# Attention output and half of the normalised input transposed by DMA in place of TensorE, with query blocks of 112

## The chip, the cores and the metric

The kernel runs on one core of one Trainium2 chip. The metric is device time in microseconds (us); lower is better. The kernel before took a median of 177.43 us over three runs (176.70 to 177.52).

## What is computed

One layer over 2048 tokens of width 448, all in bf16. The input is normalised, and two branches read the normalised rows `xn`: a sliding, dilated attention with 16 heads of 28, and a dense layer of width 1792 with gelu. The second gates the first.

```python
xn = (x - mean(x)) / sqrt(var(x) + 1e-5)
q, k, v = split_heads(xn @ wqkv)                      # 16 heads of 28
# query s sees the keys s, s-2, s-4, ..., s-14 that are not negative
s = (softmax(q . k[idx] / sqrt(28)) @ v[idx]).merge_heads() @ wo
h = gelu(xn @ w1 + b1) @ w2 + b2                      # 448 -> 1792 -> 448
out = x + s * silu(h)
```

## The kernel before, in words

Since the window steps by two, even and odd tokens never meet in the attention. The kernel lays the tokens out as two halves, first the 1024 even ones and then the 1024 odd ones (`tok`, `rows`), so that a query sees 8 neighbouring positions. All work is done in this order of tokens: 16 tiles of 128 tokens, grouped into four chunks of 512.

**The work of a tile or chunk.** A tile is loaded, its statistics are taken (`stats`, `rstds`), and VectorE writes the normalised rows into an `xn` buffer (`norm`, L359). The matmuls need the width on the partitions, so TensorE transposes each tile with four matmuls against an identity (L366), and VectorE or ScalarE copies the result from PSUM into `xnT`. From `xnT` come, chunk by chunk, q and k (`qk`, L415 and L418), and the hidden layer `h` (`ff1`, L457 and L460, gelu by ScalarE at L464). `vproj` (L435, L438) makes v for the 128 keys of one attention block. The width 448 is three times 128 and a rest of 64, and the second line number of each pair is the matmul for that rest.

**An attention block** (`attn`) holds 120 queries, the first one 128, against 128 keys; there are 17. TensorE makes the scores of 16 heads in 16 small matmuls (L526) into four PSUM banks, ScalarE takes exp (L532), VectorE multiplies by a mask (L540), and TensorE multiplies with v (L547, 16 matmuls in four groups of four), where a column of ones gives the sum. VectorE takes the reciprocal `rd` (L554) and writes the scaled output `os` (L559). Then TensorE transposes `os` with four matmuls of 112 columns (L568), and VectorE or ScalarE copies the result into `oT` (through the helper `copy`, L258 and L260). One block holds the border between the halves and has a mask of its own (`m_sp`).

**The end of a tile.** `ff2` multiplies `h` with `w2` (L483, 14 matmuls in two groups of seven), VectorE and ScalarE form the gate `g`, and `final` multiplies `oT` with `wo` (L584, four matmuls), scales and adds (L589, L594) and stores the tile through SyncE's queue (L598).

**What sets the order.** The kernel writes no order by hand. `_Plan` collects every step with its engine, an assumed cost, what it depends on, a priority and the buffers it takes; `run` then simulates these costs, and `emit` issues the steps in the order of that simulated time. Each engine, and the queue of DMAs that SyncE issues, runs its steps strictly in this order. Where a step may run on two engines (the copies), the plan also chooses the engine. The stages are added as: chunk 0's gelu layer (F), attention of chunks 0 and 1 (A), F of 1, A of 2, F of 2, A of 3, F of 3. Steps of `ff2`, `qk`, `vproj` and `final` fill the gaps between. Warm-up matmuls (L273) keep TensorE busy until the first weights are there. The bias `b1` comes in as 14 rows, `b1r`, is turned by one matmul (L625) and copied (L629); its load stands behind the hold `t_hold` in SyncE's queue, after the loads of `w1`.

Of the kernel before, what the change touches and what calls it, by code (L numbers as in the profile page):

```python
# [143 lines left out]
def kernel(  # L144
# [26 lines left out]
    GW = 4 * DH  # L171
# [3 lines left out]
    BLK = [(0, 128, 0)] + [(128 + 120 * i, 120, 120 + 120 * i) for i in range(16)]  # L175
    SPLIT = next(i for i, (q0, n, _) in enumerate(BLK) if q0 <= HALF < q0 + n)

# [16 lines left out]

    x_sb = sb("x_sb", [P, NT, D])
# [7 lines left out]
    wo = sb("wo", [P, G, D])  # L203
# [6 lines left out]
    oT = sb("oT", [P, G, S])  # L210
    ident = sb("ident", [P, P])
    eps_t = sb("eps_t", [P, 1], F32)
    m_gen = sb("m_gen", [P, 4, 120])
    m_b0 = sb("m_b0", [P, 4, 128])
    m_sp = sb("m_sp", [P, 4, 120])
    m1 = [sb(f"m1_{i}", [P, 128]) for i in range(3)]
# [7 lines left out]
    p_xn = ring("xn", 3, [P, 512])  # L224
# [3 lines left out]
    p_os = ring("os", 2, [P, D])  # L228
# [19 lines left out]
    def act(n):  # L248
        return 0.19 + n / 1200.0
# [37 lines left out]
    t_E = [plan.add("DVE", 0.08, memset("vector", e[:, :, 120:], 0.0), [t_on], prio=95) for e in p_E.bufs]  # L287

    def dma(eng, dst, src, kb, prio, deps=()):
        def fn(_):  # L290
            (nc.sync if eng == "SP" else nc.scalar).dma_start(dst, src)  # L291
# [63 lines left out]
    def norm(t, prio):  # L355
        def f1(k):
            xn = buf(p_xn, k)
            for o, i in ((xn[:, :D], x_sb[:, t, :]), (xn[:, D:], x_sb[:, t, KF:])):
                nc.vector.tensor_scalar(o, i, mv[:, t, 0:1], rstd[:, t:t + 1], op0=ALU.subtract, op1=ALU.mult)  # L359

        a = plan.add("DVE", 0.45, f1, [t_rs[t]], prio, take=(p_xn,))

        def f2(k):
            xn, tp = buf(p_xn, a), half_bank(buf(p_b, k))
            for kt in range(KT):
                nc.tensor.transpose(tp[:, kt, :], xn[:, kt * P:(kt + 1) * P], ident[:])  # L366
# [149 lines left out]
    def attn(b, prio, gate, early):  # L516
        q0, nq, k0 = BLK[b]
        m = m_b0 if b == 0 else m_sp if b == SPLIT else m_gen
# [39 lines left out]
        def f6(k):  # L558
            nc.vector.tensor_tensor(  # L559
                out=buf(p_os, k)[:nq, :].rearrange("p (h c) -> p h c", h=H),  # L560
                in0=buf(p_b, po)[:nq, :].rearrange("p (h c) -> p h c", h=H)[:, :, :DH],
                in1=buf(p_rd, r)[:nq, :].unsqueeze(2).to_broadcast((nq, H, DH)), op=ALU.mult)
        o = plan.add("DVE", dve(D), f6, [r], prio + 4, take=(p_os,), give=((p_b, po, 0), (p_rd, r, 0)))

        def f7(k):
            tp, os_ = half_bank(buf(p_b, k)), buf(p_os, o)
            for g in range(G):
                nc.tensor.transpose(tp[:GW, g, :nq], os_[:nq, GW * g:GW * (g + 1)], ident[:nq, :nq])  # L568
        tr = plan.add("PE", 0.21, f7, [o], prio + 4, take=(p_b,), give=((p_os, o, 0),), tail=0.15)

        def f8(k):
            copy(k.on, oT[:GW, :, q0:q0 + nq], half_bank(buf(p_b, tr))[:GW, :, :nq])
        t_oT[b] = plan.add(("DVE", "ACT"), (dve(4 * nq, 2), act(4 * nq)), f8, [tr], prio + 4,
                           give=((p_b, tr, 0),))
# [3 lines left out]
    def final(t, prio):  # L578
        deps = [t_oT[b] for b, (q0, nq, _) in enumerate(BLK) if q0 < (t + 1) * P and q0 + nq > t * P]

        def f1(k):
            ps = buf(p_b, k)
            for g in range(G):
                nc.tensor.matmul(ps[:, :D], oT[:GW, g, t * P:(t + 1) * P], wo[:GW, g, :],  # L584
                                 start=(g == 0), stop=(g == G - 1))
        a = plan.add("PE", pe(D, G), f1, deps + t_wo + [t_f2[min(t + 1, NT - 1)]], prio, take=(p_b,), tail=0.15)
# [26 lines left out]
    t_b1r = dma("SP", b1r[:], B_b1.rearrange("(m f) -> m f", f=P), 4, 87, [t_hold])  # L613
# [4 lines left out]
    t_wo = [dma("SP", wo[:GW, :, :], A_wo.rearrange("(g p) c -> p g c", p=GW), 392, 80, [t_hold])]  # L618
# [7 lines left out]
    a = plan.add("PE", 0.3, f1, [t_b1r, t_ident], 97, take=(p_b,), tail=0.15)  # L626
# [38 lines left out]
    project(0)  # L665
    project(1)
# [57 lines left out]
```

## Time and profile before

| | |
|---|---|
| median of three runs | 177.43 us |
| the profiled execution's own time | 178.15 us |
| its span, first to last instruction | 176.4 us |
| TensorE (PE) busy | 168.8 us, 96% |
| ScalarE (ACT) busy | 113.2 us, 64% |
| VectorE (DVE) busy | 112.4 us, 64% |
| mean granted TensorE clock | 0.993 |
| DMA | 9.12 MB, mean 52 GB/s |

The profile is of one execution, taken by the hardware profiler. The span is 1.75 us shorter than the execution's own time. PE is the matmul row, PEld the weight loads that overlap it, SPq is the queue of instructions on SyncE that issue DMAs. A line such as L366 is a line of the kernel. "Idle before" is how long the engine sat idle just before an instruction, and the arrow names what ended that. The chain of waits is followed back from the last instruction, at each step to what released it or to the instruction before it on its engine.

### The profile page before, as it was taken

To read this page: it belongs to the slowest core of one execution; us is meant where nothing else is said; L and a number is where in the kernel's file an instruction comes from. 1 tells how busy PE (TensorE), PEld (TensorE's weight loads), DVE (VectorE), ACT (ScalarE), POOL (GpSimd) and SP (SyncE) were. 2 spreads that over 40 slices of the span, in tenths; PEclk is the share of its full clock that TensorE was granted. 3 is DMA by queue.
4 is the path that set the end of the run, shared out by engine and by line. 5 is a ranking of instruction groups with operands and counts; after the bars stand their busy time and mean duration, and the time that the engine had idled before them with its cause. 6 is when DMAs were issued, how large, how long until landed. Compare 5 with 4: busy or idle time off the path is not lost.

```text
span 176.4 us, 3588 instructions
## 1 busy us (share of the span) xinstructions
PE 168.8 (96%) x1442; PEld 84.6 (48%) x1442; DVE 112.4 (64%) x305; ACT 113.2 (64%) x202; POOL 3.1 (2%) x16
## 2 busy tenths in 40 slices
PE   7998899999999999999999999999999999999990
PEld 2465335444555455434465544344565543455540
DVE  5699771877699779710699964002799892055663
ACT  2356679798847779779954289696965948811120
POOL 7000000000000000000000000000000000000000
PEclk9999999999999999999999999999999999999997
DMA  5999960000000000000101000000000010001001
GB/s 141 323 351 222 373 192 4 4 0 2 4 0 0 4 0 4 26 0 0 32 8 37 13 24 0 6 0 0 26 4 26 4 52 0 0 30 50 30 26 52
DMA packets 8604, 9.12 MB, mean 52 GB/s; under 512 B 588, under 2 KB 8076, under 8 KB 8588
## 3 DMA queue, kind: packets, MB, share of 16 engines
q1 hardware_dynamic: 7740, 8.21, 15.1%
q10 hardware_dynamic: 848, 0.69, 1.4%
q8 instruction: 11, 0.18, 0.5%
q14 instruction: 5, 0.04, 0.1%
HBM read 7.06 MB, written 1.84 MB: 50 GB/s over the span
## 4 chain that ended last, share of the span: by engine, by line
PE 86%; DMA 9%; DVE 2%; SPq 1%; issue 1%; DVEq 0%
PE bank L483 24%; PE bank L457 21%; PE bank L415 9%; PE bank L584 7%; PE bank L435 6%; DMA b1r<-in_B_b_dram 5%; PE bank L547 4%; PE bank L460 4%; DMA wraw<-in_A_wqkv_dram 3%; PE bank L526 3%; PE bank L568 3%; PE bank L418 2%; PE bank L366 1%; PE bank L438 1%; SPq L291 1%; DVE sg L589 1%
## 5 line engine op out<-in xcount | busy, mean ns | idle before, releaser
L483 PE MATMUL bank<-w,h 128*128 128x448 bf16 x224 | 46.8, 352 | 0.0
L464 ACT ACTIVATE h<-bank,b 128x512 bf16<-128x512 f32 x56 | 34.7, 688 | 8.7 <-PE bank L460 8.5
L457 PE MATMUL bank<-xnT,w 128*128 128x512 bf16 x168 | 39.1, 380 | 0.0
L532 ACT ACTIVATE E<-bank 128x480 bf16<-128x480 f32 (+1 forms) x68 | 33.3, 582 | 8.1 <-PE bank L526 8.1
L483 PEld LDWEIGHTS <-h 128*128 128x128 bf16 x224 | 20.8, 97 | 17.8
L457 PEld LDWEIGHTS <-w 128*128 128x128 bf16 x168 | 15.1, 98 | 20.1 <-issue 4.2
L415 PE MATMUL bank<-xnT,wqk 128*128 128x512 bf16 (+1 forms) x120 | 24.7, 337 | 0.0
L505 ACT ACTIVATE t<-y 128x448 f32<-128x448 f32 x16 | 9.2, 583 | 20.6 <-DVE y L499 20.6
L540 DVE TENSOR_TENSOR E<-E,m_gen 128x480 bf16<-128x480 bf16 x60 | 21.5, 401 | 1.0 <-ACT E L532 0.7
L589 DVE SCALAR_TENSOR_TENSOR sg<-bank,g 128x448 bf16<-128x448 f32 x16 | 10.0, 622 | 14.9 <-PE bank L584 14.0
L547 PEld LDWEIGHTS <-E 128*128 128x128 bf16 x272 | 12.1, 96 | 7.9 <-DVE E L540 1.5
L499 DVE TENSOR_TENSOR y<-bank,b 128x448 f32<-128x448 f32 x16 | 9.7, 619 | 8.5 <-PE bank L483 8.5
L584 PE MATMUL bank<-wo,oT 112*128 112x448 bf16 x64 | 14.6, 353 | 0.2 <-DVE y L499 0.2
L415 PEld LDWEIGHTS <-wqk 128*128 128x128 bf16 x120 | 10.3, 97 | 7.4 <-issue 1.3
L260 DVE CAST kT<-bank 128x256 bf16<-128x256 f32 (+1 forms) x6 | 3.3, 551 | 16.3 <-PE bank L418 11.8
L547 PE MATMUL bank<-v,E 128*128 128x29 bf16 x272 | 13.6, 176 | 0.0
L435 PE MATMUL bank<-wv,xnT 128*128 128x448 bf16 x51 | 11.5, 354 | 0.0
L509 DVE SCALAR_TENSOR_TENSOR g<-t,y 128x448 bf16<-128x448 f32 x16 | 9.8, 618 | 2.6 <-ACT t L505 2.6
L559 DVE TENSOR_TENSOR os<-bank,rd 120x448 bf16<-120x448 f32 (+1 forms) x17 | 10.6, 624 | 0.6
L258 ACT CAST qT<-bank 128x512 bf16<-128x512 f32 (+1 forms) x14 | 7.2, 512 | 5.0 <-PE bank L418 3.0
L330 DVE BATCH_NORM_STATS2 st<-x_sb 128x6 f32<-128x448 bf16 x16 | 9.7, 606 | 0.9 <-DMA x_sb<-in_A_x_dram 0.9
L273 PE MATMUL bank<-warm 128*128 128x512 bf16 x25 | 8.6, 509 | 1.3 <-DVE warm L265 1.3
(58 smaller groups left out, 146.3 us busy)
## 6 DMA issues: line engine op xcount, KB each, us to landing
out_dram<-o SPq DMA_DIRECT2D x16, 112.0 KB, 1.7
w<-in_B_w_dram SPq DMA_DIRECT2D x1, 1568.0 KB, 10.4
x_sb<-in_A_x_dram SPq DMA_DIRECT2D x3, 448.0 KB, 5.8
w<-in_B_w_dram SPq DMA_DIRECT2D x1, 1344.0 KB, 11.0
wraw<-in_A_wqkv_dram SPq DMA_DIRECT2D x1, 672.0 KB, 6.0
w<-in_B_w_dram SPq DMA_DIRECT2D x2, 224.0 KB, 9.6
wo<-in_A_wo_dram SPq DMA_DIRECT2D x1, 392.0 KB, 6.9
wv<-in_A_wqkv_dram ACTq DMA_DIRECT2D x1, 336.0 KB, 10.7
```

What stands on the lines that cost most here:

```text
L415: nc.tensor.matmul(ps[:, :n], wqk[:, kt, hs, :], xnT[:, kt, cs], start=start, stop=stop)
L435: nc.tensor.matmul(ps[:, :D], xnT[:, kt, k0:k0 + P], wv[:, kt, :], start=start, stop=stop)
L457: nc.tensor.matmul(ps[:], w1[:, kt, ms], xnT[:, kt, cs], start=start, stop=stop)
L464: nc.scalar.activation(buf(p_h, own, i)[:], buf(p_b, own, i)[:], ACT.Gelu_apprx_tanh, bias=b1[:, mt:mt + 1])
L483: nc.tensor.matmul(ps[:, :D], buf(*h_at[(c, mt)])[:, j * P:(j + 1) * P], w2[:, mt, :], start=(mt == 0), stop=(mt == NMT - 1))
L509: nc.vector.scalar_tensor_tensor(out=buf(p_g, k)[:], in0=buf(p_t, th)[:], scalar=1.0, in1=buf(p_y, y)[:], op0=ALU.add, op1=ALU.mult)
L532: nc.scalar.activation(buf(p_E, k)[:, :, :nq], buf(p_b, a, hl)[:, :4 * nq].rearrange("p (g q) -> p g q", g=4), ACT.Exp, scale=SCALE)
L540: nc.vector.tensor_tensor(out=E[:, :, :nq], in0=E[:, :, :nq], in1=m[:, :, :nq], op=ALU.mult)
L547: nc.tensor.matmul(ps[:, h, :DH + 1], buf(p_E, e)[:, g, :], buf(*v_at[b])[:, h, :DH + 1], start=True, stop=True)
L559: nc.vector.tensor_tensor(out=buf(p_os, k)[:nq, :].rearrange("p (h c) -> p h c", h=H), in0=buf(p_b, po)[:nq, :].rearrange("p (h c) -> p h ...
L584: nc.tensor.matmul(ps[:, :D], oT[:GW, g, t * P:(t + 1) * P], wo[:GW, g, :], start=(g == 0), stop=(g == G - 1))
L589: nc.vector.scalar_tensor_tensor(out=buf(p_sg, k)[:], in0=buf(p_b, a)[:, :D], scalar=0.5, in1=buf(p_g, t_g[t])[:], op0=ALU.mult, op1=ALU.mult)
```

## The change

Eight of the 16 tiles (8 to 15, the odd tokens) and all attention outputs are transposed by a DMA that SyncE issues (`dma_T`) in place of four TensorE matmuls and a copy from PSUM. The blocks have 112 queries in place of 120: each half of the tokens is now a block of 128 and eight of 112, which fills its 1024 exactly. There are 18 blocks, none holds the border, and the third mask goes. The `os` buffers become 512 columns wide, with the last 64 zeroed once by GpSimd; `oT` and `wo` get the layout 3 x 128 + 64 rows (the fourth group of `wo` filled up with zeros), so `final` still has four matmuls. The rings `xn` and `os` grow from 3 to 6 and from 2 to 5 buffers. The load of `b1r` no longer waits for the hold and moves ahead of the loads of `x` and `w1`; the matmul that turns it has a lower priority.

```diff
@@ -168,12 +168,13 @@
     NCH = S // CH
     TPC = CH // P
     G = 4
-    GW = 4 * DH
     HALF = S // 2
 
 
-    BLK = [(0, 128, 0)] + [(128 + 120 * i, 120, 120 + 120 * i) for i in range(16)]
-    SPLIT = next(i for i, (q0, n, _) in enumerate(BLK) if q0 <= HALF < q0 + n)
+    NQ = 112
+    BLK = []
+    for s in (0, HALF):
+        BLK += [(s, P, s)] + [(s + P + NQ * i, NQ, s + NQ * (i + 1)) for i in range((HALF - P) // NQ)]
 
     def tok(ap):
         return ap.rearrange("b (s two) d -> two (b s) d", two=2)
@@ -190,6 +191,7 @@
 
     def sb(name, shape, dt=BF16):
         return const.tile(shape, dt, name=name)
+
 
 
     x_sb = sb("x_sb", [P, NT, D])
@@ -200,20 +202,19 @@
     wv = sb("wv", [P, KT, D])
     w1 = sb("w1", [P, KT, F])
     w2 = sb("w2", [P, NMT, D])
-    wo = sb("wo", [P, G, D])
+    wo = sb("wo", [P, KT, D])
     b1r = sb("b1r", [NMT, P])
     b1 = sb("b1", [P, NMT], F32)
     b2 = sb("b2", [P, D])
     xnT = sb("xnT", [P, KT, S])
     qT = [sb(f"qT{g}", [P, S]) for g in range(G)]
     kT = [sb(f"kT{g}", [P, S]) for g in range(G)]
-    oT = sb("oT", [P, G, S])
+    oT = sb("oT", [P, KT, S])
     ident = sb("ident", [P, P])
     eps_t = sb("eps_t", [P, 1], F32)
-    m_gen = sb("m_gen", [P, 4, 120])
-    m_b0 = sb("m_b0", [P, 4, 128])
-    m_sp = sb("m_sp", [P, 4, 120])
-    m1 = [sb(f"m1_{i}", [P, 128]) for i in range(3)]
+    m_gen = sb("m_gen", [P, 4, NQ])
+    m_b0 = sb("m_b0", [P, 4, P])
+    m1 = [sb(f"m1_{i}", [P, P]) for i in range(2)]
     mv = sb("mv", [P, NT, 2], F32)
     sd = sb("sd", [P, NT], F32)
     rstd = sb("rstd", [P, NT], F32)
@@ -221,11 +222,11 @@
     def ring(name, n, shape, dt=BF16, fifo=False):
         return _Pool([sb(f"{name}{i}", shape, dt) for i in range(n)], fifo)
 
-    p_xn = ring("xn", 3, [P, 512])
+    p_xn = ring("xn", 6, [P, 512])
     p_st = ring("st", 4, [P, 6], F32)
     p_E = ring("E", 8, [P, 4, P], fifo=True)
     p_rd = ring("rd", 2, [P, H], F32)
-    p_os = ring("os", 2, [P, D])
+    p_os = ring("os", 5, [P, 512])
     p_y = ring("y", 2, [P, D], F32)
     p_t = ring("t", 2, [P, D], F32)
     p_g = ring("g", 4, [P, D])
@@ -284,13 +285,19 @@
     t_wz = [plan.add("DVE", 0.3, memset("vector", wqk[:, :, :, DH:], 0.0), [t_on], prio=98),
             plan.add("DVE", 0.1, memset("vector", wqk3[:, :, DH:], 0.0), [t_on], prio=97)]
     t_vw = [plan.add("DVE", 0.08, memset("vector", v[:, :, DH:DH + 1], 1.0), [t_on], prio=96) for v in p_v.bufs]
-    t_E = [plan.add("DVE", 0.08, memset("vector", e[:, :, 120:], 0.0), [t_on], prio=95) for e in p_E.bufs]
+    t_E = [plan.add("DVE", 0.08, memset("vector", e[:, :, NQ:], 0.0), [t_on], prio=95) for e in p_E.bufs]
 
     def dma(eng, dst, src, kb, prio, deps=()):
         def fn(_):
             (nc.sync if eng == "SP" else nc.scalar).dma_start(dst, src)
         a = plan.add(eng, 0.45, fn, [t_on] + list(deps), prio)
         return plan.add("DMA", kb / 310.0, lambda _: None, [a], prio, tail=1.7)
+
+    def dma_T(dst, src, deps, give):
+        def fn(_):
+            nc.sync.dma_start_transpose(out=dst, in_=src())
+        a = plan.add("SP", 1.3, fn, deps, 70)
+        return plan.add("DMA", 0.6, lambda _: None, [a], 70, give=(give,), tail=1.5)
 
     t_x = {}
 
@@ -359,6 +366,9 @@
                 nc.vector.tensor_scalar(o, i, mv[:, t, 0:1], rstd[:, t:t + 1], op0=ALU.subtract, op1=ALU.mult)
 
         a = plan.add("DVE", 0.45, f1, [t_rs[t]], prio, take=(p_xn,))
+        if t >= 2 * TPC:
+            t_xT[t] = dma_T(xnT[:, :, t * P:(t + 1) * P], lambda: buf(p_xn, a)[:], [a], (p_xn, a, 0))
+            return
 
         def f2(k):
             xn, tp = buf(p_xn, a), half_bank(buf(p_b, k))
@@ -515,7 +525,7 @@
 
     def attn(b, prio, gate, early):
         q0, nq, k0 = BLK[b]
-        m = m_b0 if b == 0 else m_sp if b == SPLIT else m_gen
+        m = m_b0 if q0 == k0 else m_gen
         deps = [t_k[(g, c)] for g in range(G) for c in range(k0 // P, (k0 + P - 1) // P + 1)]
         deps += [t_q[(g, c)] for g in range(G) for c in range(q0 // P, (q0 + nq - 1) // P + 1)]
 
@@ -557,21 +567,11 @@
 
         def f6(k):
             nc.vector.tensor_tensor(
-                out=buf(p_os, k)[:nq, :].rearrange("p (h c) -> p h c", h=H),
+                out=buf(p_os, k)[:nq, :D].rearrange("p (h c) -> p h c", h=H),
                 in0=buf(p_b, po)[:nq, :].rearrange("p (h c) -> p h c", h=H)[:, :, :DH],
                 in1=buf(p_rd, r)[:nq, :].unsqueeze(2).to_broadcast((nq, H, DH)), op=ALU.mult)
-        o = plan.add("DVE", dve(D), f6, [r], prio + 4, take=(p_os,), give=((p_b, po, 0), (p_rd, r, 0)))
-
-        def f7(k):
-            tp, os_ = half_bank(buf(p_b, k)), buf(p_os, o)
-            for g in range(G):
-                nc.tensor.transpose(tp[:GW, g, :nq], os_[:nq, GW * g:GW * (g + 1)], ident[:nq, :nq])
-        tr = plan.add("PE", 0.21, f7, [o], prio + 4, take=(p_b,), give=((p_os, o, 0),), tail=0.15)
-
-        def f8(k):
-            copy(k.on, oT[:GW, :, q0:q0 + nq], half_bank(buf(p_b, tr))[:GW, :, :nq])
-        t_oT[b] = plan.add(("DVE", "ACT"), (dve(4 * nq, 2), act(4 * nq)), f8, [tr], prio + 4,
-                           give=((p_b, tr, 0),))
+        o = plan.add("DVE", dve(D), f6, [r] + t_os, prio + 4, take=(p_os,), give=((p_b, po, 0), (p_rd, r, 0)))
+        t_oT[b] = dma_T(oT[:, :, q0:q0 + nq], lambda: buf(p_os, o)[:nq, :], [o], (p_os, o, 0))
         return exps
 
 
@@ -580,10 +580,10 @@
 
         def f1(k):
             ps = buf(p_b, k)
-            for g in range(G):
-                nc.tensor.matmul(ps[:, :D], oT[:GW, g, t * P:(t + 1) * P], wo[:GW, g, :],
-                                 start=(g == 0), stop=(g == G - 1))
-        a = plan.add("PE", pe(D, G), f1, deps + t_wo + [t_f2[min(t + 1, NT - 1)]], prio, take=(p_b,), tail=0.15)
+            for kt in range(KT):
+                nc.tensor.matmul(ps[:, :D], oT[:, kt, t * P:(t + 1) * P], wo[:, kt, :],
+                                 start=(kt == 0), stop=(kt == KT - 1))
+        a = plan.add("PE", pe(D, KT), f1, deps + t_wo + [t_f2[min(t + 1, NT - 1)]], prio, take=(p_b,), tail=0.15)
 
         def f2(k):
             nc.vector.scalar_tensor_tensor(out=buf(p_sg, k)[:], in0=buf(p_b, a)[:, :D], scalar=0.5,
@@ -610,12 +610,13 @@
     load_x(4, 4, 91, "SP", [t_hold])
     t_w1 = [dma("SP", w1[:, 0:3, :], ktiles(B_w1[0:KF, :]), 1344, 90, [t_hold])]
     t_w1 += [dma("SP", w1[64 * i:64 * i + 64, 3, :], B_w1[KF:D, :], 224, 89 - i, [t_hold]) for i in range(2)]
-    t_b1r = dma("SP", b1r[:], B_b1.rearrange("(m f) -> m f", f=P), 4, 87, [t_hold])
+    t_b1r = dma("SP", b1r[:], B_b1.rearrange("(m f) -> m f", f=P), 4, 95)
     load_x(8, 4, 86, "SP", [t_hold])
     load_x(12, 4, 85, "SP", [t_hold])
     t_w2 = [dma("SP", w2[:], B_w2.rearrange("(m p) c -> p m c", p=P), 1568, 82, [t_hold])]
     t_b2 = dma("SP", b2[:], B_b2.rearrange("(o d) -> o d", o=1).to_broadcast((P, D)), 112, 81, [t_hold])
-    t_wo = [dma("SP", wo[:GW, :, :], A_wo.rearrange("(g p) c -> p g c", p=GW), 392, 80, [t_hold])]
+    t_wo = [dma("SP", wo[:, 0:3, :], ktiles(A_wo[0:KF, :]), 336, 80, [t_hold]),
+             dma("SP", wo[:64, 3, :], A_wo[KF:D, :], 56, 79, [t_hold])]
 
     for t in range(TPC, NT):
         stats(t)
@@ -623,13 +624,13 @@
 
     def f1(k):
         nc.tensor.transpose(buf(p_b, k)[:].bitcast(BF16)[:, :NMT], b1r[:], ident[:NMT, :NMT])
-    a = plan.add("PE", 0.3, f1, [t_b1r, t_ident], 97, take=(p_b,), tail=0.15)
+    a = plan.add("PE", 0.3, f1, [t_b1r, t_ident], 60, take=(p_b,), tail=0.15)
 
     def f2(_):
         nc.vector.tensor_copy(b1[:], buf(p_b, a)[:].bitcast(BF16)[:, :NMT])
-    t_b1 = plan.add("DVE", 0.17, f2, [a], 97, give=((p_b, a, 0),))
-
-    masks = ((m_gen, m1[0], 120, -1, 8), (m_b0, m1[1], 128, 7, 0), (m_sp, m1[2], 120, -1, 8))
+    t_b1 = plan.add("DVE", 0.17, f2, [a], 60, give=((p_b, a, 0),))
+
+    masks = ((m_gen, m1[0], NQ, NQ + 7 - P, P - NQ), (m_b0, m1[1], P, 7, 0))
     t_mask = []
     for m, w, n, lo, hi in masks:
         def fn(_, m=m, w=w, n=n, lo=lo, hi=hi):
@@ -638,12 +639,7 @@
                                     pattern=[[-1, n]], channel_multiplier=1)
             nc.gpsimd.affine_select(out=w[:, :n], in_=w[:, :n], compare_op=ALU.is_ge, fill=0.0, base=hi,
                                     pattern=[[1, n]], channel_multiplier=-1)
-            if m is m_sp:
-                q0, _, k0 = BLK[SPLIT]
-                j = HALF - q0
-                nc.gpsimd.affine_select(out=w[:, j:n], in_=w[:, j:n], compare_op=ALU.is_ge, fill=0.0,
-                                        base=k0 - HALF, pattern=[[0, n - j]], channel_multiplier=1)
-        t_m = plan.add("POOL", 1.2 if m is m_sp else 0.9, fn, [t_ident], prio=75)
+        t_m = plan.add("POOL", 0.9, fn, [t_ident], prio=75)
 
         def fn(_, m=m, w=w, n=n):
             nc.vector.tensor_copy(m[:], w[:, :n].unsqueeze(1).to_broadcast((P, 4, n)))
@@ -663,6 +659,8 @@
         batch(vs[:2], vs[2:], p - 0.1)
 
     project(0)
+    t_os = [plan.add("POOL", 0.6, memset("gpsimd", o[:], 0.0), [t_xT[3]]) for o in p_os.bufs]
+    t_wo.append(plan.add("POOL", 0.4, memset("gpsimd", wo[64:, 3, :], 0.0), [t_xT[3]]))
     project(1)
     for c, what in ((0, "F"), (0, "A"), (1, "A"), (1, "F"), (2, "A"), (2, "F"), (3, "A"), (3, "F")):
         if what == "A":
```

The plan is computed anew, so the order on every engine moves. Two places show what matters below.

SyncE's queue, from the last loads on. Before, it holds only stores (`out`) after the loads:

```order
L291 DMA x_sb_61<-in_A_x_dram 128x4x448 x2
L291 DMA w2_68<-in_B_w2_dram 128x14x448
L291 DMA b2_72<-in_B_b2_dram 128x448
L291 DMA wo_69<-in_A_wo_dram 112x4x448
L598 DMA out_0_dram<-o0_123 128x448
L598 DMA out_0_dram<-o1_124 128x448
```

After, transposes of `xn` (tiles 8, 9, 10, 11, then 12 to 15) and of `os` (blocks 0 to 3) stand there, in this order:

```order
L298 DMA_TRANSPOSE xnT_73<-xn2_94 128x4x128
L298 DMA_TRANSPOSE xnT_73<-xn3_95 128x4x128
L298 DMA_TRANSPOSE xnT_73<-xn4_96 128x4x128
L298 DMA_TRANSPOSE xnT_73<-xn5_97 128x4x128
L298 DMA_TRANSPOSE oT_82<-os0_112 128x4x128
L298 DMA_TRANSPOSE xnT_73<-xn0_92 128x4x128
L298 DMA_TRANSPOSE xnT_73<-xn1_93 128x4x128
L298 DMA_TRANSPOSE oT_82<-os1_113 128x4x112
L298 DMA_TRANSPOSE xnT_73<-xn2_94 128x4x128
L298 DMA_TRANSPOSE oT_82<-os2_114 128x4x112
L298 DMA_TRANSPOSE xnT_73<-xn3_95 128x4x128
L298 DMA_TRANSPOSE oT_82<-os3_115 128x4x112
```

What moved: the queue now carries 26 transposes, the first 13 of them ahead of the first store. The one for block 2 (`os2`, 112 columns) is the tenth. Each waits for VectorE's write of its source and for the DMA that stood eight places ahead.

VectorE's order from the end of block 0's attention on. The names: `rd` reciprocals, `os` attention output, `E` the masked exponentials, `xn` the normalised rows. Before:

```order
L554 RECIPROCAL rd0_109<-bank3_166 128x16
L559 TENSOR_TENSOR os0_111<-bank3_166,rd0_109 128x448
L260 COPY oT_82<-bank1_164 112x4x128
L540 TENSOR_TENSOR E4_105<-E4_105,m_gen_85 128x4x120
L540 TENSOR_TENSOR E5_106<-E5_106,m_gen_85 128x4x120
L540 TENSOR_TENSOR E6_107<-E6_107,m_gen_85 128x4x120
L260 CAST qT2_76<-bank3_166 128x512
L540 TENSOR_TENSOR E7_108<-E7_108,m_gen_85 128x4x120
L554 RECIPROCAL rd1_110<-bank6_169 120x16
L559 TENSOR_TENSOR os1_112<-bank6_169,rd1_110 120x448
L540 TENSOR_TENSOR E0_101<-E0_101,m_gen_85 128x4x120
L260 COPY oT_82<-bank6_169 112x4x120
```

After:

```order
L564 RECIPROCAL rd0_110<-bank4_171 128x16
L569 TENSOR_TENSOR os0_112<-bank4_171,rd0_110 128x448
L550 TENSOR_TENSOR E4_106<-E4_106,m_gen_85 128x4x112
L550 TENSOR_TENSOR E5_107<-E5_107,m_gen_85 128x4x112
L366 TENSOR_SCALAR xn0_92<-x_sb_61,mv_89,rstd_91 128x448
L366 TENSOR_SCALAR xn0_92<-x_sb_61,mv_89,rstd_91 128x64
L550 TENSOR_TENSOR E6_108<-E6_108,m_gen_85 128x4x112
L550 TENSOR_TENSOR E7_109<-E7_109,m_gen_85 128x4x112
L366 TENSOR_SCALAR xn1_93<-x_sb_61,mv_89,rstd_91 128x448
L366 TENSOR_SCALAR xn1_93<-x_sb_61,mv_89,rstd_91 128x64
L261 CAST qT1_75<-bank7_174 128x512
L564 RECIPROCAL rd1_111<-bank4_171 112x16
```

What moved: the copy into `oT` that followed each block's transpose is gone from VectorE, and the normalisation of tiles 12 and 13 (`xn0`, `xn1`) stands between the masks of block 1.

## Prediction

> **What bounds the kernel now.** I read the page first: busy time, the 40 slices, the chain of waits.
>
> ```profile
> PE 168.8 (96%) x1442; PEld 84.6 (48%) x1442; DVE 112.4 (64%) x305; ACT 113.2 (64%) x202; POOL 3.1 (2%) x16
> ...
> PE 86%; DMA 9%; DVE 2%; SPq 1%; issue 1%; DVEq 0%
> ```
>
> TensorE (PE) is busy for 168.8 of 176.4 us, and 86% of the chain that ended last is PE. So what leaves PE shortens the kernel, as long as no other engine is late in its place. Where PE is not busy is told by the stages (the view of busy time by windows) and by PE's own waits:
>
> ```profile
> 0.00:18.40 18.40, 15.81 (x103) 8.54 (x103) 13.86 (x62) 7.93 (x18) 3.09 (x16) 1.00 0.90 263
> ...
> 30.90:71.00 40.10, 39.77 (x459) 20.87 (x460) 32.56 (x88) 31.57 (x60) 0.00 (x0) 1.00 0.01 2
> ```
> ```profile
> PE bank L625 <- DMA b1r<-in_B_b_dram: 1.3, 1, 1.3
> PE bank L273 <- DVE warm L265: 1.3, 1, 1.3
> PE bank L568 <- DVE os L559: 0.3, 1, 0.3
> PE bank L584 <- DVE y L499: 0.2, 1, 0.2
> ```
>
> The columns of the windows are PE, PEld, DVE, ACT and POOL busy, then the granted clock. PE is idle until its first warm-up, for 1.3 us at the matmul that turns `b1r`, and otherwise only in the tail. In the first attention stage (30.9 to 71.0) it is busy for 39.77 of 40.10 us, with DVE at 81% and ACT at 79%.
>
> **What leaves PE.** A matmul's own duration covers its latency, so I take the price from the chain in order of time, which shows what four of them add to PE's row of work:
>
> ```profile
> 50.43 0.33 PE bank L366 x4
> 50.76 0.57 PE bank L435 x3
> 51.32 0.21 PE bank L568 x4
> ...
> 53.53 0.29 PE bank L547 x12
> 53.82 0.48 PE bank L438 x4
> ...
> 55.76 0.32 PE bank L526 x16
> ...
> 72.96 0.35 PE bank L568 x4
> ...
> 88.25 0.23 PE bank L366 x4
> ```
>
> Output transposes: 17 groups of four. On the chain most take 0.21 as here, some 0.35, and all of L568 together is 2.6% of it, by the chain's shares by line:
>
> ```profile
> by line: PE bank L483 24.3%; PE bank L457 21.2%; PE bank L415 9.2%; PE bank L584 6.8%; PE bank L435 5.8%; DMA b1r<-in_B_b_dram 5.4%; PE bank L547 4.2%; PE bank L460 4.2%; DMA wraw<-in_A_wqkv_dram 3.4%; PE bank L526 2.9%; PE bank L568 2.6%;
> ```
>
> The groups of instructions have their busy time, mean and count:
>
> ```profile
> L568 PE MATMUL bank<-ident,os 120*112 120x120 bf16 (+1 forms) x68 | 6.7, 221 | 0.3 <-DVE os L559 0.3
> L366 PE MATMUL bank<-ident,xn 128*128 128x128 bf16 x64 | 5.3, 219 | 0.0
> ```
>
> The bounds are 17 x 0.21 = 3.6 us and the 6.7 us of the group's busy time. I take 4.6 us, 2.6% of 176.4, since that is what the chain holds.
>
> Transposes of `xn`: tiles 8 to 15, eight groups of four. By the cheaper row that is 8 x 0.23 = 1.8 us, by the group's busy time half of 5.3 = 2.6 us. I take 1.8.
>
> The Trainium skill, page "VectorE: DVE Perf Modes", section "The three transpose paths", gives 390 ns for a 128x128 transpose on TensorE. The rows differ: in a full stream one costs 0.23 / 4 = 58 ns. By the page's price the two removals would be worth 100 x 0.39 = 39 us; the row decides.
>
> **What comes onto PE.** One more block: 16 score matmuls 0.32, four groups of four L547 at 0.29 / 3, so 0.39, and one more v: three L435 0.57 and one L438 0.12. Together 1.4 us. Scores of 112 columns in place of 120 may give back up to 17 x 0.32 x 8/120 = 0.4 us; I take none. `final` keeps four matmuls, over 128 rows in place of 112: no more columns, so nothing.
>
> **The load of `b1r`.** The chain and the issues at the start:
>
> ```profile
> 1.70 5.99 DMA wraw<-in_A_wqkv_dram
> ...
> 8.23 0.61 SPq L291
> 8.88 9.47 DMA b1r<-in_B_b_dram
> 18.39 0.18 PE bank L625
> 18.57 1.40 PE bank L457 x6
> ```
> ```profile
> 9.81 0.82 PE L415 MATMUL bank<-xnT,wqk 128*128 128x256 bf16 x6
> ```
> ```profile
> w<-in_B_w_dram SPq DMA_DIRECT2D x2, 224.0 KB, 9.6
> ...
> wraw<-in_A_wqkv_dram SPq DMA_DIRECT2D x2, 56.0 KB, 5.7
> ```
>
> The 1.3 us wait goes. Next late is `w1`: its last piece is issued at 8.23 and lands 9.6 us later, at 17.8. Without the wait PE would begin L457 at 18.39 - 1.3 = 17.1 and reach the first matmul that needs this piece 1.40 us later, at 18.5, so the whole wait can go. But `b1r`'s matmul now stands before the first projection (L415, at 9.81), with four warm-up matmuls between them, and its load behind the three of `wraw`. Those begin to issue at 1.70; at some 0.5 us each `b1r` is issued at 3.2, and with the 5.7 us of the small loads ahead of it it lands at 8.9. Its 0.18 us and four warm-ups (512 columns, as L457, of which six take 1.40) end at 10.0, which is 0.2 late. I take 1.0 us saved, with bounds 0 and 1.3.
>
> **What is hidden.** VectorE and ScalarE lose 17 copies into `oT` and eight into `xnT`, and gain a block's exps and masks, neither of which PE waits for now. GpSimd zeroes five `os` buffers and a piece of `wo` once tile 3 is transposed; it was busy for 3.1 us in all and has the whole gelu stage, until 30.9, before an `os` is written. Were that cover gone, block 0's `os` would wait.
>
> **The new waits.** A transposing DMA does not occur in this trace. Its issue on SyncE's queue is bounded by the cheapest and the dearest issue here, its landing by a store of nearly its size:
>
> ```profile
> 16.83 3.74 SPq L291 DMA_DIRECT2D b<-in_B_b_dram  x1
> 20.61 0.43 SPq L291 DMA_DIRECT2D wo<-in_A_wo_dram  x1
> ```
> ```profile
> out_dram<-o SPq DMA_DIRECT2D x16, 112.0 KB, 1.7
> ```
>
> So 0.4 to 3.7 us an issue, one after another in the queue. The tightest place is `final` of tile 1, which needs block 2's output: in the order of SyncE's queue the tenth transpose. PE's order from the last matmul of chunk 0's gelu layer to that `final` holds 112 L526, 100 L547, 42 L483, 30 L415, 27 L435, 9 L438, 8 L418 and one L584 group. With the rows above and these
>
> ```profile
> 43.71 0.66 PE bank L415 x3
> ...
> 47.06 1.33 PE bank L483 x7
> ...
> 57.48 0.54 PE bank L418 x4
> ...
> 66.18 0.76 PE bank L584 x4
> ```
>
> that is 2.2 + 2.4 + 8.0 + 6.6 + 5.1 + 1.1 + 1.1 + 0.8 = 27.3 us. The first transpose's source, tile 8, is ready after the last gelu, a table load, the root, the reciprocal and the normalisation:
>
> ```profile
> L464 ACT ACTIVATE h<-bank,b 128x512 bf16<-128x512 f32 x56 | 34.7, 688 | 8.7 <-PE bank L460 8.5
> ```
> ```profile
> 30.63 1.28 ACT L340 ACT_TABLE_LOAD   x1
> 31.93 0.30 ACT L340 ACTIVATE sd<-mv,eps_t 128x8 f32<-128x8 f32 x1
> ```
> ```profile
> 31.59 0.59 DVE L359 TENSOR_SCALAR xn<-x_sb,mv,rstd 128x448 bf16<-128x448 bf16 x2
> 32.26 0.20 DVE L343 RECIPROCAL rstd<-sd 128x8 f32<-128x8 f32 x1
> ```
>
> 0.69 + 1.28 + 0.30 + 0.20 + 0.59 = 3.1 us. That leaves 27.3 - 3.1 = 24.2 us for ten issues and one landing of 1.7: PE never waits while an issue takes at most 22.5 / 10 = 2.25 us. I take about 1.3, the middle of 0.43 and 3.74 by ratio, and so no wait. Later places are looser: the fourth transpose (tile 11) and the fifth (block 0) have their readers only 5 to 6 us of PE work sooner, and from block 8 on some 30 us of PE work lie between a block and its `final`. Queued behind a transpose that waits are the stores, for which only the three `o` buffers wait.
>
> **The sum.** 4.6 + 1.8 + 1.0 - 1.4 = 6.0 us less. The profiled execution would go from 178.15 to 172.15, its span from 176.4 to 170.4; the median shown is 0.72 under the profiled execution, so the forecast is 177.43 - 6.0 = 171.4 us. With the terms' bounds the gain lies between 3.6 + 1.8 + 0 - 1.4 = 4.0 and 6.7 + 2.6 + 1.3 - 1.0 = 9.6 us, so 167.8 to 173.4; the far end needs all terms to err alike, and I use 168.5.
>
> **Rival 1, slower: the transposes come one by one and late.** At 3.74 us an issue the tenth lands 37.4 + 1.7 = 39.1 us after tile 8 is ready, 14.9 us too late: PE stands at the `final` of tile 1, and all scores and masks behind it too. 171.4 + 14.9 = 186.3 us. It decides from 2.25 us an issue, and the gain is gone at (22.5 + 6.0) / 10 = 2.85. For it: the row of 3.74 is also of 128 partitions by 448 columns. Against it: every other issue here is under 0.65. Chance 0.14.
>
> The Trainium skill, page "VectorE: DVE Perf Modes", section "The three transpose paths", gives 1309 ns for a 128x128 DMA transpose, and its section "Rules for kernel authors" says to use TensorE where the result may go to PSUM, which speaks against this change: four such pieces would make an estimated 5.2 us each, 52 + 1.7 - 24.2 = 30 us late, about 201 us. The Trainium skill, page "DMA: Bandwidth & Descriptors", section "Latency and other measured facts", has 261 GB/s for transposes, by which the 128 KB would take an estimated 0.5 us and nothing would wait. No run here shows either yet.
>
> **Rival 2: ACT and VectorE hold the first attention stage.** It now takes nine blocks, not eight, with less on PE. If its 40.1 us do not shrink, the seven output groups in it (the window view, by that line: 2.77 us busy) are not gained: 171.4 + 2.8 = 174.2 us. For it: 79 and 81% busy, in order, with casts between the exps. Against it: PE's waits above show none for ACT. Chance 0.10.
>
> ```profile
> 30.90:71.00 40.10, 2.77 (x28) 2.24 (x28) 1.00 0.01 2
> ```
>
> **Rival 3: no change.** All attention stages run at the pace of exps and masks; 4.6 and 1.8 are not gained: 171.4 + 6.4 = 177.8 us. Same signs as rival 2. Chance 0.05.
>
> **How the numbers follow.** The forecast has 0.71. Range 168.5 to 175.5: it holds the forecast and rival 2 with some room, about 0.8. Half a percent, 0.9 us, is about what a measurement of this kernel can tell. Faster by more: the forecast and rival 2, 0.81; within: rival 3, 0.05; slower: rival 1, 0.14.
>
> **What would show it.** In the profile after: no L568 group and half of the `xn` transposes; no PE wait at `b1r` over 0.3 us; issues of transposes on SPq under 2.25 us; PE's waits without one for a DMA; PE busy near 164 us at a share of 96%. Wrong if PE waits for `oT` or `xnT` (rival 1), or if PE's idle time grows in the first attention stage with no DMA late (rivals 2 and 3).

## The result, and the profile after

| | before | changed |
|---|---|---|
| median of four runs each | 177.34 us | 172.72 us |
| ratio, 95% interval | | 0.974 (0.971 to 0.977) |
| profiled execution, its span | 178.15, 176.4 us | 172.8, 171.0 us |
| PE busy | 168.8 us | 162.3 us |

The change makes the kernel 4.6 us faster. The forecast was 6.0 us faster, 171.4 us, with a range of 168.5 to 175.5. The page after, with the lines that answer to those of before:

```profile
PE 162.3 (95%) x1362; PEld 79.6 (47%) x1377; DVE 106.3 (62%) x290; ACT 111.1 (65%) x202; POOL 4.9 (3%) x18
...
PE 80%; DVE 9%; DMA 4%; ACT 3%; issue 2%; SPq 0%; ACTq 0%; DVEq 0%
```

By these rows PE lost 6.5 us of work, the span 5.4, and PE's idle time grew from 7.6 to 8.7 us. But the profile after lacks 15 records of matmuls that the kernel issues (160 of 168 of L467, 65 of the 72 of L425 with 512 columns), and the one before lacks none. In experiment 4, which leaves PE's work as it is, 13 missing records go with 1.0 us less of busy time. So an estimate for PE's loss is 5.3 us, near the 5.0 of the sum, with as much idle time as before. The chain of waits has 9% DVE and 3% ACT now. Where PE waits, in the view of its waits:

```profile
PE bank L274 <- DVE warm L266: 1.3, 1, 1.3
PE bank L376 <- ACT h L474: 1.0, 2, 0.8
PE bank L626 <- DMA b1r<-in_B_b_dram: 0.8, 1, 0.8
PE bank L467 <- issue: 0.3, 2, 0.2
PE bank L425 <- issue: 0.2, 1, 0.2
```

No wait is for a transpose, `xnT` or `oT`. The wait of 1.3 us at `b1r` is gone, and two others are there: 0.8 us at its new place, and 1.0 us for the first gelus. The first cost little. The first projection begins at 10.07 us against 9.81 before, and the gelu layer's first matmul at 17.14 against 18.50:

```profile
10.07 0.82 PE L425 MATMUL bank<-xnT,wqk 128*128 128x256 bf16 x6
...
17.14 1.46 PE L467 MATMUL bank<-xnT,w 128*128 128x512 bf16 x5
```

The second is explained on ScalarE (from the view of all waits), and by VectorE's and ScalarE's order of time around it:

```profile
ACT L474 <- DVE b L630: 3.4, 1, 3.4
```
```profile
20.21 0.59 DVE L337 BATCH_NORM_STATS2 st<-x_sb 128x6 f32<-128x448 bf16 x1
20.84 0.18 DVE L338 BATCH_NORM_AGGREGATE mv<-st 128x2 f32<-128x6 f32 x1
20.94 0.14 DVE L630 CAST b<-bank 128x14 f32<-128x14 bf16 x1
```
```profile
21.16 1.28 ACT L474 ACT_TABLE_LOAD   x1 [3.44 <-DVE b L630]
22.45 2.42 ACT L474 ACTIVATE h<-bank,b 128x512 bf16<-128x512 f32 x4
```

`b1r` is turned by 9.3 us, but the copy of `b1`, now with a low priority, stands behind the statistics of eight tiles in VectorE's order and runs at 20.9. Before, it ran at 18.6. ScalarE waits 3.4 us for it, the first gelu begins at 22.45 (20.33 before), and PE waits for PSUM banks that the gelus have yet to read. The chain that ended last goes this way too. From 8.4 to 21.2 us nearly all of it is VectorE's statistics, normalisation and copies, then it goes over the gelus to PE:

```profile
20.30 0.52 DVE st L337
21.16 1.28 ACT L474
22.45 0.22 ACT h L474
...
23.77 0.61 PE bank L376 x8
```

The transposes themselves, from SyncE's queue and the list of DMA issues (the last column is the median us from issue to landing):

```profile
34.30 5.23 SPq L298 DMA_TRANSPOSE xnT<-xn  x4
41.10 1.19 SPq L298 DMA_TRANSPOSE oT<-os  x1
42.38 2.53 SPq L298 DMA_TRANSPOSE xnT<-xn  x2
```
```profile
oT<-os SPq DMA_TRANSPOSE x18, 2.4
...
xnT<-xn SPq DMA_TRANSPOSE x8, 2.5
```

One takes 1.2 us of the queue and lands 2.4 us after its issue began.

### The profile page after: what moved, and what is told of

It is laid out like the page before. It is cut to its first block, busy times and chain, and to the rows that moved or that the text cites. A ratio compares the mean times of both kernels' runs of the same rounds, so it can differ in the third digit from the quotient of the medians.

```text
span 171.0 us, 3505 instructions
## 1 busy us (share of the span) xinstructions
PE 162.3 (95%) x1362; PEld 79.6 (47%) x1377; DVE 106.3 (62%) x290; ACT 111.1 (65%) x202; POOL 4.9 (3%) x18
## 4 chain that ended last, share of the span: by engine, by line
PE 80%; DVE 9%; DMA 4%; ACT 3%; issue 2%; SPq 0%; ACTq 0%; DVEq 0%
PE bank L493 25%; PE bank L467 19%; PE bank L425 8%; PE bank L584 7%; PE bank L445 6%; PE bank L557 5%; PE bank L470 4%; DMA wraw<-in_A_wqkv_dram 4%; PE bank L536 3%; DVE st L337 2%; DVE xn L366 2%; PE bank L428 2%; PE bank L448 1%; ACT E L542 1%; DVE mv L338 1%
## 5 line engine op out<-in xcount | busy, mean ns | idle before, releaser
L542 ACT ACTIVATE E<-bank 128x448 bf16<-128x448 f32 (+1 forms) x72 | 33.8, 558 | 9.3 <-PE bank L536 9.2
L467 PE MATMUL bank<-xnT,w 128*128 128x512 bf16 x160 | 38.3, 380 | 0.6 <-issue 0.3
L467 PEld LDWEIGHTS <-w 128*128 128x128 bf16 x168 | 15.2, 98 | 21.1 <-issue 5.1
L425 PE MATMUL bank<-xnT,wqk 128*128 128x512 bf16 (+1 forms) x113 | 23.9, 334 | 0.5 <-issue 0.2
L550 DVE TENSOR_TENSOR E<-E,m_gen 128x448 bf16<-128x448 bf16 x64 | 22.2, 385 | 1.3 <-ACT E L542 1.0
L515 ACT ACTIVATE t<-y 128x448 f32<-128x448 f32 x16 | 9.2, 577 | 17.5 <-DVE y L509 17.5
L584 PE MATMUL bank<-wo,oT 128*128 128x448 bf16 x64 | 14.6, 353 | 0.1
L425 PEld LDWEIGHTS <-wqk 128*128 128x128 bf16 x120 | 10.2, 97 | 7.5 <-issue 1.7
L445 PE MATMUL bank<-wv,xnT 128*128 128x448 bf16 x54 | 12.3, 353 | 0.0
L569 DVE TENSOR_TENSOR os<-bank,rd 112x448 bf16<-112x448 f32 (+1 forms) x18 | 11.2, 624 | 1.0
L259 ACT CAST qT<-bank 128x512 bf16<-128x512 f32 (+1 forms) x15 | 7.9, 524 | 4.7 <-PE bank L428 3.2
L259 ACT CAST v<-bank 128x448 bf16<-128x448 f32 x13 | 6.9, 536 | 5.5 <-PE bank L445 3.7
L366 DVE TENSOR_SCALAR xn<-x_sb,mv,rstd 128x448 bf16<-128x448 bf16 (+1 forms) x32 | 9.0, 343 | 0.1
```

What stands on the lines that cost most here:

```text
L259: nc.scalar.copy(o, i)
L425: nc.tensor.matmul(ps[:, :n], wqk[:, kt, hs, :], xnT[:, kt, cs], start=start, stop=stop)
L445: nc.tensor.matmul(ps[:, :D], xnT[:, kt, k0:k0 + P], wv[:, kt, :], start=start, stop=stop)
L467: nc.tensor.matmul(ps[:], w1[:, kt, ms], xnT[:, kt, cs], start=start, stop=stop)
L542: nc.scalar.activation(buf(p_E, k)[:, :, :nq], buf(p_b, a, hl)[:, :4 * nq].rearrange("p (g q) -> p g q", g=4), ACT.Exp, scale=SCALE)
L550: nc.vector.tensor_tensor(out=E[:, :, :nq], in0=E[:, :, :nq], in1=m[:, :, :nq], op=ALU.mult)
```

## The experiments

Theory: the transposes on the DMA cost PE nothing, and what is missing against the forecast was lost at the bias `b1`. Rival: the loss sits in the attention stages, whose order is denser. A second question was the price of each part, and a third the point from which rival 1 of the prediction would decide. Each edit but those of 10 and 11 makes the plan compute a new order, so a part taken back alone also carries the differences of that order. The experiments ran in three groups, each with runs of the kernel before, whose medians were 177.31, 177.31 and 177.36 us.

**1. The bias put back.**

```diff
-    t_b1r = dma("SP", b1r[:], B_b1.rearrange("(m f) -> m f", f=P), 4, 95)
+    t_b1r = dma("SP", b1r[:], B_b1.rearrange("(m f) -> m f", f=P), 4, 87, [t_hold])
-    a = plan.add("PE", 0.3, f1, [t_b1r, t_ident], 60, take=(p_b,), tail=0.15)
+    a = plan.add("PE", 0.3, f1, [t_b1r, t_ident], 97, take=(p_b,), tail=0.15)
-    t_b1 = plan.add("DVE", 0.17, f2, [a], 60, give=((p_b, a, 0),))
+    t_b1 = plan.add("DVE", 0.17, f2, [a], 97, give=((p_b, a, 0),))
```

> The changed kernel with the b1r load and its matmul and copy put back where they stood before (behind the hold, priority 97). Theory: moving the load earned nothing, since the wait at b1r came back as waits of 0.8 us at the new place and 1.0 us for the first gelus; so within 0.5 us of the changed kernel's 172.7. Rival: the move earned its 1.0 us as in the sum and the shortfall lies in the attention stages; then 173.7 us or more.

172.63 us (172.15 to 173.47), the same as 172.72 within the spread. Moved in the way of the change, the load earned nothing that can be measured.

**2. The matmul later, the copy earlier.** The load stays early; the steps are added after chunk 0's projections.

```diff
-    a = plan.add("PE", 0.3, f1, [t_b1r, t_ident], 60, take=(p_b,), tail=0.15)
+    a = plan.add("PE", 0.3, f1, [t_b1r, t_ident, t_q[(0, 0)]], 97, take=(p_b,), tail=0.15)
-    t_b1 = plan.add("DVE", 0.17, f2, [a], 60, give=((p_b, a, 0),))
+    t_b1 = plan.add("DVE", 0.17, f2, [a], 97, give=((p_b, a, 0),))
```

> The changed kernel with the b1r load early as it is, but its matmul after chunk 0's first projections and its copy on VectorE at high priority. Theory: the wait of 0.8 us before the first projection, the 3.4 us that ScalarE waits for b1 and the 1.0 us that PE then waits for the first gelus all go: 171.0 to 172.0 us. Rival: w1's landing or VectorE's statistics take their place; then 172.7 us, no change against the changed kernel.

171.83 us (ratio to before 0.968, 0.965 to 0.971), 0.8 us under experiment 1 and 0.9 under the changed kernel. Both waits are gone, as its PE waits show:

```profile
PE bank L274 <- DVE warm L266: 1.2, 1, 1.2
PE bank L584 <- DVE os L569: 0.5, 1, 0.5
PE bank L467 <- issue: 0.3, 2, 0.2
```

PE's busy time in the first 31 us, the first number behind the comma (window views of four kernels: before, changed, the bias put back, this one), tells the same of the changed kernel and this one:

```profile
0.00:31.00 31.00, 28.41 (x188) 14.07 (x190) 21.45 (x87) 18.25 (x34) 3.09 (x16) 1.00 0.76 228
```
```profile
0.00:31.00 31.00, 27.80 (x176) 14.23 (x179) 22.64 (x89) 17.47 (x33) 4.92 (x18) 1.00 0.73 228
```
```profile
0.00:31.00 31.00, 28.57 (x197) 14.29 (x200) 22.40 (x89) 18.35 (x34) 4.94 (x18) 1.00 0.73 228
```
```profile
0.00:31.00 31.00, 29.65 (x198) 14.76 (x200) 22.35 (x89) 18.34 (x34) 4.94 (x18) 1.00 0.70 228
```

The changed kernel does less on PE by 31 us (27.80) than the kernel before (28.41). With the matmul late and the copy early it does 29.65, all but the start-up. From 31 to 166 us the two are busy for 133.83 and 133.45 of 135.00, so what separates them arises at the start. With the bias put back it does 28.57, in an execution that was the fastest of its six (172.15 us).

**3. The copy earlier, the matmul where the change puts it.**

```diff
-    t_b1 = plan.add("DVE", 0.17, f2, [a], 60, give=((p_b, a, 0),))
+    t_b1 = plan.add("DVE", 0.17, f2, [a], 97, give=((p_b, a, 0),))
```

> The changed kernel with the bias copy on VectorE at high priority; its matmul stays ahead of the first projection. Theory: the 1.0 us that PE waits for the first gelus goes, the 0.8 us at the matmul stays: 171.7 to 172.3 us. Rival: the copy now waits for b1r ahead of a copy of the weights on VectorE, and the first projection starts later: 172.7 us or more.

171.94 us. So this one edit is worth about 0.8 us. The first projection begins no earlier than in the changed kernel (10.20 us against 10.07), the first gelu does (19.17 against 22.45). The expectation erred in one point: no wait for `b1r` is left in this profile, where PE's next waits after the warm-up are 0.5 and 0.3 us; the projections' order moved as well.

**4. The same bias in the kernel before.** The two steps stand after chunk 0's projections, as in experiment 2.

```diff
-    t_b1r = dma("SP", b1r[:], B_b1.rearrange("(m f) -> m f", f=P), 4, 87, [t_hold])
+    t_b1r = dma("SP", b1r[:], B_b1.rearrange("(m f) -> m f", f=P), 4, 95)
-    a = plan.add("PE", 0.3, f1, [t_b1r, t_ident], 97, take=(p_b,), tail=0.15)
+    a = plan.add("PE", 0.3, f1, [t_b1r, t_ident, t_q[(0, 0)]], 97, take=(p_b,), tail=0.15)
```

> The kernel before with only the bias changed: its load early, its matmul after chunk 0's first projections, its copy at high priority. Theory: the 1.3 us that PE waits at b1r go and nothing is late next, since w1's last piece lands before PE needs it: 176.0 us. Rival: w1 or the statistics on VectorE take the wait's place: 177.3 us.

176.65 us against 177.36 (ratio 0.996, 0.994 to 0.998): 0.7 us, half of the 1.3 that PE waited at `b1r`. So the wait of before could go, but by its own length it was overpriced.

**5 and 6. Each transpose back on TensorE alone.** The first takes the DMA out of `norm`, the second puts four matmuls and a copy for each block into `attn`.

```diff
-        if t >= 2 * TPC:
-            t_xT[t] = dma_T(xnT[:, :, t * P:(t + 1) * P], lambda: buf(p_xn, a)[:], [a], (p_xn, a, 0))
-            return
```

> The changed kernel with tiles 8 to 15 transposed by TensorE again; the attention output stays with the DMA. Theory: the eight groups cost PE the 1.8 us of the sum: 174.5 us. Rival: they only filled gaps in PE's row, so at most 173.2 us.

```diff
-        t_oT[b] = dma_T(oT[:, :, q0:q0 + nq], lambda: buf(p_os, o)[:nq, :], [o], (p_os, o, 0))
...
+            for kt in range(KT):
+                nc.tensor.transpose(tp[:, kt, :nq], os_[:nq, P * kt:P * (kt + 1)], ident[:nq, :nq])
...
+            copy(k.on, oT[:, :, q0:q0 + nq], half_bank(buf(p_b, tr))[:, :, :nq])
```

> The changed kernel with the attention output transposed by TensorE again (18 groups of four, over 128 columns each in the layout of three times 128 and a rest) and copied from PSUM; tiles 8 to 15 stay with the DMA. Theory: 18 x 0.27 = 4.9 us on PE: 177.6 us. Rival: part of it hides in waits that the DMA version has elsewhere, 175 us.

With `xn` back 176.64 us, with `os` back 177.13. The outputs cost 4.4 us, near the expected 4.9. But `xn` costs 3.9, twice the expected 1.8, and PE waits at those transposes:

```profile
PE bank L373 <- ACT h L471: 1.1, 2, 0.9
PE bank L373 <- ACT xnT L259: 0.7, 1, 0.7
PE bank L373 <- DVE xnT L261: 0.6, 2, 0.4
```

The first of these waits is in the changed kernel too (1.0 us, at L376). The other two, 1.3 us for copies into `xnT`, are new. To see whether the prices hang on the trouble at the start, both were repeated without it.

**7 and 8. The same two edits on top of experiment 2.**

> The version with b1r's matmul late (171.83), with tiles 8 to 15 on TensorE again. Without the waits at the start, theory: the groups cost the 2.8 us of busy time of half the xn transposes: 174.6 us. Rival: the waits that came with them before (1.3 us, for the copies into xnT) belong to them: 175.5 us or more.

> The version with b1r's matmul late (171.83), with the attention output on TensorE again. Theory: the price of 4.4 us does not hang on the start: 176.2 us. Rival: without the waits at the start the groups fill gaps, 175 us or less.

With `xn` back 172.80 us, with `os` back 175.93, against 171.83. The outputs cost 4.1 us again; `xn` costs 1.0, under both expectations, and those waits are gone. The start itself is not where the two prices of `xn` differ. PE's work in the first 31 us hardly changes with the edit on either base (27.97 us against 27.80 in experiment 5, 29.64 against 29.65 here). Of the 2.9 us between the prices, 1.3 are the waits for the copies, which stand at 35.8 and from 85.7 to 86.7 us; where the rest lies is open.

**9. Blocks of 112 alone.** The kernel before with 18 blocks and two masks, all transposes on TensorE.

```diff
-    BLK = [(0, 128, 0)] + [(128 + 120 * i, 120, 120 + 120 * i) for i in range(16)]
+    NQ = 112
+    for s in (0, HALF):
+        BLK += [(s, P, s)] + [(s + P + NQ * i, NQ, s + NQ * (i + 1)) for i in range((HALF - P) // NQ)]
```

> The kernel before with blocks of 112 queries and nothing else: 18 blocks, all transposes on TensorE, b1r as before. Theory: one more block costs PE its 1.4 us and one more output group 0.3 us: 179.0 us. Rival: narrower scores and masks give it back, 177.4 us.

179.59 us against 177.31 (ratio 1.013, 1.010 to 1.016): 2.3 us, 0.6 more than expected. PE's busy time in this profile is 168.7 us, as before, but 14 records of matmuls are missing in it, which by the figures of experiment 4 hide an estimated 1.1 us. So how the 2.3 us split into work and waits can't be read from it.

This kernel and that of experiment 1 have the same blocks and the same handling of the bias, and differ in where the transposes run and what comes with that (the rings, the layout of `oT` and `wo`). 179.59 - 172.63 = 7.0 us is thus the price of both transposes taken together; the sum had 4.6 + 1.8, and 0.3 for the group of the 18th block, 6.7.

**10 and 11. Each DMA transpose issued twice, and three times.** The extra ones write to spare buffers; the planned order stays. The second kernel has `range(2)`.

```diff
         def fn(_):
-            nc.sync.dma_start_transpose(out=dst, in_=src())
+            s = src()
+            nc.sync.dma_start_transpose(out=dst, in_=s)
+            for _ in range(1):
+                e = extra[0].pop(0)
+                extra[0].append(e)
+                nc.sync.dma_start_transpose(out=e[:, :, :s.shape[0]], in_=s)
```

> The changed kernel with each DMA transpose issued twice, the second into a spare buffer, in the same planned order; 26 issues of 1.2 us more on SyncE's queue. Theory (a threshold in the queue): tile 8's issue begins at 34.3 us and the tenth pair's first half ends 19 issues later, 34.3 + 19 x 1.2 = 57.1, lands 1.2 us after that, before PE reaches the final of tile 1 at 59.5: no change, 172.7 us. Rival: every transpose in flight costs something (DMA traffic, landing times that grow), so already 1 to 3 us slower.

> The changed kernel with each DMA transpose issued three times, two into spare buffers; 3.6 us of SyncE's queue for each, near the 3.74 us of the rival in the prediction. Theory: the tenth's first issue ends at 34.3 + 28 x 1.2 = 67.9 and lands at 69.1, 9.6 us after PE reaches the final of tile 1 at 59.5; PE waits there and the time is 182 us, slower than the kernel before. Rival: the buffers and the order have more room than counted, or the stall shifts later work into gaps, so that less than half of it shows: under 177.5 us.

Twice 176.90 us (ratio to before 0.998, 0.995 to 1.001), three times 190.24 (1.073, 1.069 to 1.077). Each has one long wait, at a `final`:

```profile
PE bank L591 <- DMA oT<-os: 2.8, 1, 2.8
```
```profile
PE bank L591 <- DMA oT<-os: 14.4, 1, 14.4
```

The first expectation was missed by the spacing, not by the place. In SyncE's queue of the first kernel the first and the tenth transpose that count were issued at

```profile
33.80 1.31 SPq L301 DMA_TRANSPOSE xnT<-xn  x1
...
59.30 1.21 SPq L301 DMA_TRANSPOSE oT<-os  x1
```

so 25.5 us apart, or 2.83 each, where 2 x 1.2 had been counted: the pairs take 2.6 with the gaps between them, and two transposes took over 2.0. In the second kernel these are

```profile
36.12 1.29 SPq L301 DMA_TRANSPOSE xnT<-xn  x1
...
73.36 1.21 SPq L301 DMA_TRANSPOSE oT<-os  x1
```

4.14 each. In the changed kernel the first is issued at 34.3 and PE reaches the `final` of tile 1 at 59.5, 25.2 us later. The wait should then be nine spacings and a landing of 2.4 less 25.2: 25.5 + 2.4 - 25.2 = 2.7 and 37.2 + 2.4 - 25.2 = 14.4 us, and it is 2.8 and 14.4. The second expectation had counted 9.6 us of wait, with 3.6 us for three transposes where they took 4.14. This is a queue with a threshold, not a cost for each transpose: the landing stays at 2.4 us, and PE waits for a transpose at no other place. Against the changed kernel the two lost 4.2 and 17.5 us, more than the waits. The granted clock, the first number behind the five engines, in the windows around the wait of the first kernel,

```profile
58.90:61.80 2.90, 0.08 (x5) 0.03 (x2) 1.48 (x4) 0.03 (x1) 0.00 (x0) 0.83 0.30 50
61.80:66.00 4.20, 3.87 (x23) 1.62 (x25) 0.69 (x1) 0.63 (x2) 0.00 (x0) 0.50 0.50 101
66.00:70.00 4.00, 4.00 (x43) 1.47 (x40) 3.48 (x9) 3.09 (x7) 0.00 (x0) 0.80 0.45 90
70.00:74.00 4.00, 3.95 (x44) 2.00 (x42) 3.61 (x9) 3.34 (x8) 0.00 (x0) 1.00 0.45 103
```

is 0.50 over the 4.2 us after it. In windows of 0.5 us it falls at about 60.8, 1.8 us after PE's last matmul and with the wait still on, and is back at 1.00 at about 67.6, 5.8 us after the wait ended. At half the clock these 5.8 us can cost up to 2.9, so the clock can account for the rest of the 4.2. The times of single executions agree: two of the ten of this kernel had a mean granted clock of 0.998 and 0.999 and took 175.63 and 176.02 us, about 172.7 and the wait; the others, at 0.981 to 0.990, took 175.81 to 178.06.

**12. Four more tiles on the DMA.** On top of experiment 2:

```diff
-    p_xn = ring("xn", 6, [P, 512])
+    p_xn = ring("xn", 8, [P, 512])
-        if t >= 2 * TPC:
+        if t >= TPC:
```

> The kernel with b1r's matmul late and its copy early, and tiles 4 to 7 given to the DMA as well (xn ring of 8). Theory: four more groups leave PE, 4 x 0.23 = 0.9 us under the version with b1r's matmul late: about 170.6 us. Rival: at that time the queue still issues weights and the loads of w2 are in flight, tile 7's transpose is late for chunk 1's projections and PE waits: no gain or slower than that version.

171.14 us (ratio to before 0.966, 0.964 to 0.968), the fastest median here; the interval overlaps that of experiment 2, so the further 0.7 us are likely and not certain. Its profile shows no wait of PE for a DMA.

## Why the prediction was right, and where not

**The sign and the mechanism** were right. PE was the bound, the four matmuls of each transpose left it, and no transpose on the DMA was waited for.

**The issue of a transpose**, taken as 1.3 us between 0.4 and 3.7, is 1.2; the landing, taken as 1.7 from a store, is 2.4.

**Rival 1's mechanism** held, at the place that the prediction named. Its numbers were partly luck. The prediction put the begin of a wait at 2.25 us an issue and the loss of the whole gain at 2.85, and at a spacing of 2.83 the kernel is indeed level with before. But it counted ten issues and a landing of 1.7 against 24.2 us, by which the wait at 2.83 would be 5.8 us; it was 2.8, since nine spacings and a landing of 2.4 stand against 25.2. By these the wait begins at (25.2 - 2.4) / 9 = 2.5 us, an estimate, as no run lies between 1.3 and 2.83. The clock after the wait, which the price lacked, and a gain of 4.6 in place of 6.0 made up for the difference. At 4.14 the kernel is 7% slower than before.

**The Trainium skill's** 1309 ns for a 128x128 DMA transpose (page "VectorE: DVE Perf Modes", section "The three transpose paths"), times four, an estimate of 5.2 us, does not hold here: 1.2 us of the queue and 2.4 to land for four such pieces.

**Output transposes**, 4.6 us in the sum: 4.1 and 4.4 measured. **Transposes of `xn`**, 1.8 us: 1.0 on one base, 3.9 on another. **The block more**, 1.4 us: 2.3 alone on the old kernel. With the bias handled alike on both sides, experiment 4 to experiment 2, the transposes and the blocks together gave 176.65 - 171.83 = 4.8 us; the sum had 4.6 + 1.8 - 1.4 = 5.0. Taken one by one the parts do not add up to that: 4.1 + 1.0 - 2.3 is 2.8. Taken in the order of first the blocks (experiment 9), then both transposes at once (experiments 9 and 1), the two steps are 2.3 us more and 7.0 less, where the sum with the 18th group had 1.7 and 6.7. On this path the pair of transposes was priced well and the block 0.6 too low. The price of one transpose taken back alone carries the new order that the plan makes for each kernel; how much of it, is open.

**The load of `b1r`**, 1.0 us with bounds 0 and 1.3, is the term that failed: it earned nothing that can be measured (experiment 1). The prediction looked at the load and the matmul, and that part came out. It allowed 0.2 us for the new place, and the first projection began 0.26 late, though PE waited 0.8 there; it had L457 begin at 17.1, and its counterpart L467 began at 17.14. What it did not follow is the third step, the copy on VectorE whose priority the same edit lowered. That copy's place in VectorE's new order, behind eight tiles' statistics, would have told it. With the copy early the gain is there: 0.8 us under the changed kernel with that edit alone (experiment 3), 0.8 under the kernel with the bias put back when the matmul is late too (experiment 2). This term makes up 1.0 of the 1.4 us between forecast and result. The sign that PE would wait no more than 0.3 us at `b1r` failed with it.

**Rivals 2 and 3** fell. The first attention stage did not shrink, 39.9 us after 40.1, which rival 2 took as its condition. But it now holds nine blocks, and PE was busy for 39.5 of the 39.9, so it was not ScalarE or VectorE that held it.

```profile
31.06:71.00 39.94, 39.53 (x454) 19.94 (x458) 33.27 (x88) 31.38 (x63) 0.00 (x0) 1.00 0.27 57
```

## What to carry to other kernels

Here, work that left the bounding engine for a DMA queue was free up to a point that can be counted beforehand: the queue's place of the result times the issue time, plus a landing, against the bounding engine's work until its reader. When a step's priority is changed, follow all its parts to the last engine: here a copy of 0.14 us, moved behind the statistics, cost as much as the earlier load could earn. In a kernel whose order is planned anew, a part taken back alone measures that order as well (1.0 us on one base, 3.9 on another), so take such a price on more than one base. And count the records before busy times are compared: 13 missing matmuls were worth 1.0 us here.

## What the runs showed of the hardware

A transposing DMA of 128 or 112 rows by 512 columns of bf16, from SBUF to SBUF, took 1.2 us of SyncE's queue (1.18 to 1.45 over 26 of them) and landed 2.3 to 4.0 us after its issue began. Doubling and tripling their number left the median landing at 2.4 to 2.5.

One wait of 2.8 us on PE was enough for a granted clock of 0.50, for 6.8 us (60.8 to 67.6) in experiment 10; it began 1.8 us after PE's last matmul. In experiment 11, with a wait of 14.4 us, it began 4.1 us after PE's last matmul (at 65.5) and ended 3.4 us after the wait (at 79.1). The Trainium skill, page "TensorE: Matmul & The Clock Gate", section "Why this matters for your kernels", puts the limit for such gaps at about 3 us; the trace of experiment 10 shows the drop in a gap just under it.
